# Fewer transposes for returning maxima, an earlier slot table and x, and late work moved between VectorE and GpSimd

## The chip, the cores and the metric

The kernel runs on one core of a Trainium2 chip. The engines are TensorE (matmuls and transposes, PE in the profile, with PEld its weight loads), VectorE (DVE), ScalarE (ACT), GpSimd (POOL) and SyncE (SP, which here only issues transfers). The metric is the device time of one execution in microseconds; less is better. Three executions of the kernel before took 757.74, 759.35 and 760.75 us (median 759.35).

## The reference

Masked attention with locality-sensitive buckets, followed by a mixture of experts with one expert per token. B, H, S, D = 4, 8, 768, 64; the experts see 3072 tokens of 512 values, 8 experts, hidden width 1024.

```python
q_bits = (einsum('bhsd,dk->bhsk', q, proj) > 0)        # 6 signs; bucket = their number; k likewise
mask   = q_bucket[..., :, None] == k_bucket[..., None, :]
scores = where(mask, q @ k.T / sqrt(D), -1e9)
scores = scores - max(scores, -1)
attn   = exp(scores) / (sum(exp(scores), -1) + 1e-9)
x      = (attn @ v), heads side by side                # 3072 x 512
logits = x @ w_gate + modality_bias[modality_id]
e      = argmax(logits);  gate = softmax(logits)[e]
out    = gate * (relu(x @ w1[e]) @ w2[e])              # per token, with its own expert
```

## The kernel before

**Attention.** The 32 heads are done as 16 pairs of two. For each pair, `turn` transposes q and k, `signs` multiplies them by the projection and compares, so that 12 extra rows beside the 64 of each operand carry the bucket mask, and `residues` splits the operands for two-pass products. `maxp` takes the maximum of each query's row of scores: three matmuls per tile pair and head write the banks of `psm` (two of them), VectorE reduces each (L346, L352). Queries lie in six tiles of 128. After the second tile pair (four tiles) and after the third (two tiles), L360 gathers the maxima, ScalarE spreads each over 32 columns (L363), and a closure for `maxp_back` is put into the list `late`.

`maxp_back` (L371 to L378) turns the maxima back, so that they lie along the columns of the operand: one transpose for each query tile (L374), then one instruction per head (L377) that adds them to 12 rows of the operand, and one (L378) that writes `lone`, the flag of a query that no key matches. Of each 32 rows of the spread, two halves of REP = 16 are filled for two heads. `lone` is a tile of the pool `flags`, two buffers. `vsums` writes a small matrix `vs`, which multiplied by `lone` gives the mean of v to lone queries (L457, the first instruction of each pair's `weigh`).

`score` makes the scores (L410, L411), the exponentials on ScalarE (L430, L444) and running sums over the key tiles (L447): on GpSimd, but for the second head of pair 15 (`spd=(15,)`), which is on VectorE. `weigh` multiplies by v (L463). `sums` adds the running sums over partitions (L486) one pair later, and `finish`, once for each of the four batches, makes reciprocals, router logits and the routing table (`tab`, by GpSimd's scatters, L784). `finish_x` writes x to DRAM, six tiles per batch, each four transposes (L548), a scaling on VectorE (L550) and a store (L552).

TensorE's order is written by hand: for each pair and each of six key tiles there is a string of letters (PLAN, PLAN0 for pair 0, LAST for pair 15). S is a score step, M a maximum step, T turn or signs, R residues, A two key tiles of weighing, B one call from `late`, Q the row sums of the pair before, v and V the sums of v, F, f, e, E steps of `finish`, x and y one tile of `finish_x` (x in pairs 6, 10, 14, y in pairs with i % 4 == 3). The other engines' orders come from a scheduler that takes, at each moment of its model, the earliest-written instruction that is ready. In pair 0 the orders of VectorE, ScalarE and GpSimd are also by hand (FIRST).

**Seam.** In pair 15, at its second key tile, `early_slots` (L833) works out on VectorE which two slots of 496 tokens of batches 0 to 2 can be done first; it works in a PSUM tile of `ps_x`. Then the experts' part begins: `gather` (L936) reads the slot's rows of `tab` (L941), clamps the token numbers on GpSimd (L947) and issues four indirect gathers of x (L949). `load` (L919, L923) reads the expert's weights in eight pieces of 512 KB, into four buffers, the first behind the last x store of batch 2. `split` makes each piece into an upper half (ScalarE, L929) and its residue (L933): on VectorE, but for odd pieces below 8, on GpSimd. `xprep` turns the gathered tokens (L967, four columns of four transposes each; two columns before and two behind the last weighing), copies them (L970) and takes their residues (L974). `gemm1` (L985 to L987) and `gemm2` (L1026 to L1028) follow, with batch 3's `finish` woven in.

**Experts.** After the two early slots come four more big ones, a small one and a tiny one, and the results are scattered to `out` (L1096).

Of the kernel before, what the change touches and what calls it, by code (L numbers as in the profile page):

```python
# [31 lines left out]

GROUP = 2
# [27 lines left out]
def host_consts():  # L61
    thr = np.zeros((4, 32, 3, 2), np.float32)
    for g in range(4):
        for t in range(3):
            query = (t != g // 2) if t < 2 else g % 2 == 0
            thr[g, 0:6 if query else 0, t, 0] = -TINY
            thr[g, 6:6 if query else 12, t, 0] = -TINY
            thr[g, :, t, 1] = -BIG if query else 1.0
    return {
        "c_thr": thr.reshape(128, 6),  # L70
        "c_id": np.eye(128, dtype=np.float32),
        "c_tri": np.triu(np.ones((128, 128), np.float32), 1),
    }
# [20 lines left out]
def attention(ctx, actx, tc, a, x_d, l_d, route=None, setup=None, before_last=None):  # L94
# [18 lines left out]
    flags = actx.enter_context(tc.tile_pool(name="flags", bufs=2))  # L113
# [34 lines left out]
    thr = const.tile([P, 6], F32, name="thr")  # L148
    nc.scalar.dma_start(out=thr, in_=a["c_thr"])
    load(0, (1,))  # L150
# [181 lines left out]
    def maxp(i, late, heads=(0, 1)):  # L332
# [4 lines left out]
        if "lone" not in t:  # L337
            t["lone"] = flags.tile([P, S], F32R, name="lone")
        mx = sm.tile([P, NT, nh, 2], F32, name=f"mx{nh}")
        for qt in range(0, NT, 2):  # L340
# [27 lines left out]
            late.append(partial(maxp_back, t, heads, rows, nm, n, slice(first * P, (qt + 2) * P)))  # L368
            yield

    def maxp_back(t, heads, rows, nm, n, cs):  # L371
# [17 lines left out]
    def vsums(i):  # L389

        a2, vs, share = st[i]["va"], vsb[i % 2], 1.0 if i else REP / 32
        vp = ps_x.tile([P, MAIN], F32, name="psx")
        nc.tensor.matmul(vp[:, 0:P], ones32, a2.rearrange("p h d -> p (h d)"), start=True, stop=True)
        for h in range(2):
            r = slice(64 * h, 64 * h + 64)
            nc.scalar.mul(vs[r, r], vp[r, r], share)
        for h in range(2):
            r = slice(64 * h, 64 * h + 64)
            lo = slice(64 * h + 32, 64 * h + 64)
            nc.vector.scalar_tensor_tensor(out=vs[lo, r], in0=vp[lo, r], scalar=share, in1=vs[lo, r].bitcast(F32), op0=ALU.mult, op1=ALU.subtract)  # L400
# [12 lines left out]
    def score(i):  # L413
# [22 lines left out]
        for kt in range(NT):  # L436
# [8 lines left out]
            if kt > 0:  # L445
                for h in range(2):
                    marks["add"] = (nc.vector if h and i in CFG["spd"] else nc.gpsimd).tensor_tensor(out=t["sp"][:, h], in0=(t["pb"][0] if kt == 1 else t["sp"])[:, h], in1=pb[:, h], op=ALU.add).ins  # L447
            yield

    def weigh():  # L450

        for i in range(NPR):
            t = st[i]
            t["u"] = [ps_u.tile([P, MAIN], F32, name=f"psu{j}") for j in range(2)]
            for part in range(2):
                w = COLS[part].stop - COLS[part].start
                nc.tensor.matmul(t["u"][part][:, 0:w], vsb[i % 2], t["lone"][:, COLS[part]], start=True, stop=False, skip_group_check=True)  # L457
# [128 lines left out]
    with tc.manual_schedule(engines={mybir.EngineType.PE}):  # L586
# [23 lines left out]
        for i in range(NPR):  # L610
# [8 lines left out]
            for kt in range(NT):  # L619
                if i == NPR - 1 and kt == 1:  # L620
                    before_last(ps_x.tile([P, MAIN], F32, name="psx"))
# [3 lines left out]
                for c in (PLAN0 if i == 0 else LAST if i == NPR - 1 else PLAN)[kt]:  # L625
# [30 lines left out]
                    elif c == "x" and i % 4 == 2 or c == "y" and i % 4 == 3:  # L656
# [38 lines left out]
def router(ctx, tc, a, x_d, tab):  # L695
# [137 lines left out]
    def early_slots(sp):  # L833
# [51 lines left out]
def experts(ctx, tc, a, x_d, tab, out, ps_x, idents, fold, marks):  # L885
# [40 lines left out]
    def split(r, n):  # L926
# [6 lines left out]
        (nc.gpsimd if n < 8 and n % 2 else nc.vector).tensor_tensor(out=lo, in0=r, in1=hi.bitcast(F32), op=ALU.subtract)  # L933
        return hi, lo

    def gather(s):  # L936
# [4 lines left out]
        nc.sync.dma_start(out=tb[:, 0:n], in_=tab[bass.ds(o, n * P), :].rearrange("(a p) w -> p a w", p=P))  # L941
# [10 lines left out]
    def xprep(s, xg, dst):  # L952
# [11 lines left out]
        for c in range(4):  # L964
# [9 lines left out]
            nc.vector.tensor_tensor(out=xl[:, c, 0:SL], in0=tp[:, 0:SL], in1=xh[:, c, 0:SL].bitcast(F32), op=ALU.subtract)  # L974
# [222 lines left out]
def body(tc, a, out):  # L1197
# [4 lines left out]
    with ExitStack() as ctx, ExitStack() as actx:  # L1202
        route, early_slots, late_slots, setup = router(ctx, tc, a, x_d, tab)
        finish, finish_x, ps_x, idents, fold, marks = attention(ctx, actx, tc, a, x_d, None, route, setup, lambda sp: eslot.append(early_slots(sp)))
# [41 lines left out]
```

## Time and profile before

| | us |
|---|---|
| median of 3 executions | 759.35 |
| the profiled execution | 760.22 |
| its span, first to last instruction | 758.1 |
| TensorE busy (modelled) | 738.9 |
| VectorE busy | 499.9 |
| GpSimd busy | 440.9 |
| ScalarE busy | 363.8 |

The span has three parts: the start up to about 50 us, the pairs up to about 450 us, the experts after that. Engine times are sums over the span, so they say nothing of one part alone; the timeline gives each instruction's start, length and, in brackets, the idle time before it and what ended that. [...]

### The profile page before, as it was taken

How to read it: one execution, taken by the hardware profiler on the slowest of the kernel's cores; microseconds unless marked ns; L12 is line 12 of the kernel's file. 1: busy time of each engine (PE TensorE's matmuls, PEld its weight loads, DVE VectorE, ACT ScalarE, POOL GpSimd, SP SyncE). 2: the span in 40 equal slices, each digit the busy share in tenths (PEclk: the TensorE clock that was granted, in tenths of full speed). 3: DMA queues.
4: the chain of work that ended last, by engine and by line, in shares of the span. 5: the costliest groups of instructions: out<-in, count | busy, mean ns of one | idle time of the engine just before them, and what ended most of it. 6: DMA issues, size and time to landing. Idle time of an engine off the chain costs nothing.

```text
span 758.1 us, 12219 instructions
## 1 busy us (share of the span) xinstructions
PE 738.9 (97%) x4308; PEld 523.4 (69%) x4308; DVE 499.9 (66%) x878; ACT 363.8 (48%) x649; POOL 440.9 (58%) x339
## 2 busy tenths in 40 slices
PE   6899999999999999999999999999999999999995
PEld 3556576566666657666666656888888877788884
DVE  6997779789877887977987877654343442334423
ACT  5446565555555555556465454343343432424333
POOL 8598779769888769887869984712222202202011
PEclk9999999999999999999999999999999999999998
DMA  9464455345676435664324163556544764434332
GB/s 187 116 142 109 113 122 140 83 106 116 111 131 162 105 91 133 121 157 124 92 69 85 61 199 112 115 207 185 159 137 139 250 214 147 141 123 139 96 113 82
DMA packets 105832, 99.26 MB, mean 131 GB/s; under 512 B 62594, under 2 KB 82978, under 8 KB 105760
## 3 DMA queue, kind: packets, MB, share of 16 engines
q1 hardware_dynamic: 99616, 83.79, 43.6%
q0 software_dynamic: 4832, 12.94, 4.9%
q10 hardware_dynamic: 1312, 1.65, 0.9%
q8 instruction: 36, 0.59, 0.4%
q14 instruction: 36, 0.29, 0.2%
HBM read 59.33 MB, written 12.94 MB: 95 GB/s over the span
## 4 chain that ended last, share of the span: by engine, by line
PE 81%; issue 9%; DMA 3%; POOL 2%; SPq 1%; DVE 1%; ACT 1%; POOLq 0%; ACTq 0%
PE psu L463 17%; PE pss L410 9%; PE pss L411 8%; PE psm L344 5%; PE hps L985 5%; PE hps L986 5%; PE hps L987 5%; PE yps L1026 4%; PE yps L1027 4%; PE yps L1028 4%; PE psm L350 3%; PE psx L303 2%; PE psx L486 2%; PE psx L548 2%; PE psu L220 1%
## 5 line engine op out<-in xcount | busy, mean ns | idle before, releaser
L447 POOL TENSOR_TENSOR sp<-sp,pb 128x768 f32<-128x768 f32 x124 | 225.3, 1851 | 14.1 <-ACT pb L444 13.4
L346 DVE TENSOR_REDUCE mx<-psm 128x1 f32<-128x512 f32 x192 | 130.0, 687 | 22.2 <-PE psm L344 19.1
L430 ACT ACTIVATE pb<-pss 128x512 f32<-128x512 f32 x186 | 111.5, 600 | 58.7 <-PE pss L411 50.2
L463 PE MATMUL psu<-pb,vt 128*64 128x512 f32 (+1 forms) x768 | 136.1, 497 | 0.0
L933 DVE TENSOR_TENSOR w<-raw,w 128x1024 fp32r<-128x1024 f32 x52 | 66.9, 1287 | 97.9 <-ACT w L929 97.3
L463 PEld LDWEIGHTS psu<-pb,vt 128*64 128x64 f32 x768 | 51.3, 137 | 70.6 <-issue 60.9
L929 ACT CAST w<-raw 128x1024 fp32r<-128x1024 f32 x56 | 58.5, 1047 | 81.4 <-PE yps L1028 76.7
L444 ACT ACTIVATE pb<-pss 128x512 f32<-128x512 f32 x93 | 55.6, 598 | 82.3 <-PE pss L411 80.0
L1096 POOL DMA_INDIRECT out<-y,tb x25 | 24.6, 984 | 104.1 <-ACT y L1095 100.4
L447 POOL TENSOR_TENSOR sp<-pb,pb 128x768 f32<-128x768 f32 x31 | 56.2, 1835 | 45.2 <-ACT pb L444 45.2
L1026 PE MATMUL yps<-w,hl 128*128 128x512 f32 x200 | 79.5, 397 | 0.0
L1027 PE MATMUL yps<-w,hh 128*128 128x512 f32 x200 | 78.1, 391 | 0.0
L1028 PE MATMUL yps<-w,hh 128*128 128x512 f32 x200 | 78.0, 390 | 0.0
L949 POOL DMA_INDIRECT xg<-x_d,tb x17 | 18.4, 1084 | 98.1 <-DMA tb<-tab 94.4
L985 PE MATMUL hps<-xh,w 128*128 128x496 f32 x192 | 74.4, 388 | 0.0
L986 PE MATMUL hps<-xl,w 128*128 128x496 f32 x192 | 73.8, 384 | 0.0
L987 PE MATMUL hps<-xh,w 128*128 128x496 f32 x192 | 73.8, 384 | 0.0
L410 PE MATMUL pss<-m_0g,s_0g 128*128 128x512 f32 (+1 forms) x186 | 69.2, 372 | 0.0
L991 DVE SCALAR_TENSOR_TENSOR hl<-hps,hh 128x496 fp32r<-128x496 f32 x48 | 32.4, 674 | 53.0 <-ACT hh L990 52.9
L352 DVE TENSOR_REDUCE mx<-psm 128x2 f32<-128x512 f32 x96 | 66.1, 688 | 1.0
L410 PE MATMUL pss<-m_1g,s_1g 128*128 128x512 f32 (+1 forms) x186 | 65.7, 353 | 0.2 <-ACT pb L430 0.2
L990 ACT ACTIVATE hh<-hps 128x496 fp32r<-128x496 f32 x48 | 28.1, 585 | 78.5 <-PE hps L987 76.1
(267 smaller groups left out, 1419.7 us busy)
## 6 DMA issues: line engine op xcount, KB each, us to landing
raw<-moe_w SPq DMA_DIRECT2D x56, 512.0 KB
vt<-v SPq DMA_DIRECT2D x16, 384.0 KB
qk<-q SPq DMA_DIRECT2D x31, 192.0 KB
qk<-k SPq DMA_DIRECT2D x31, 192.0 KB
x_d<-xs SPq DMA_DIRECT2D x18, 256.0 KB
tw<-moe_w SPq DMA_DIRECT2D x2, 2048.0 KB
m_0g<-m_0g SPq DMA_DIRECT2D x16, 192.0 KB
s_0g<-s_0g SPq DMA_DIRECT2D x16, 192.0 KB
```

Source lines behind the costliest of these rows:

```text
L346: marks["m"] = nc.vector.tensor_reduce(out=mx[:, qt + j, hi, 0:1], in_=mp, axis=AX.X, op=ALU.max).ins
L410: nc.tensor.matmul(out, t["s1"][h][:, ks], t["m1"][h][:, cs], start=True, stop=False)
L430: marks["p"] = nc.scalar.activation(t["pb"][kt][:, h, 0:MAIN], sp, AF.Exp, scale=0.125).ins
L447: marks["add"] = (nc.vector if h and i in CFG["spd"] else nc.gpsimd).tensor_tensor(out=t["sp"][:, h], in0=(t["pb"][0] if kt == 1 else t["s ...
L463: marks["u", kt] = nc.tensor.matmul(t["u"][part][64 * h:64 * h + 64, 0:w], t["v"][:, h, kt], t["pb"][kt][:, h, COLS[part]], start=False, s ...
L933: (nc.gpsimd if n < 8 and n % 2 else nc.vector).tensor_tensor(out=lo, in0=r, in1=hi.bitcast(F32), op=ALU.subtract)
L985: nc.tensor.matmul(hps, lo[:, c, fs], xh[:, c, 0:SL], start=(c == 0), stop=False)
L986: nc.tensor.matmul(hps, hi[:, c, fs], xl[:, c, 0:SL], start=False, stop=False)
L987: nc.tensor.matmul(hps, hi[:, c, fs], xh[:, c, 0:SL], start=False, stop=(c == 3))
L1026: nc.tensor.matmul(yps[g], hl[fc][:, gs], hi[:, fb], start=(fc == 0), stop=False)
L1027: nc.tensor.matmul(yps[g], hh[fc][:, gs], lo[:, fb], start=False, stop=False)
L1028: nc.tensor.matmul(yps[g], hh[fc][:, gs], hi[:, fb], start=False, stop=(fc == 7))
```

## The change

The diff has three parts.

First, the returning maxima. ScalarE's spread L363 now fills 16 of each 32 columns once per tile and head, so that one tile of 128 columns holds two query tiles, and `maxp_back` makes one transpose for two of them. Rows 0 to 63 then carry one tile and rows 64 to 127 the other. For two heads there is one addition per head and tile parity u (four, each over every second tile) and one flag instruction per u; pair 0, which does its heads one by one, keeps its transposes and its addition and has two flag instructions of 32 rows. `lone` becomes two fixed tiles that GpSimd clears at the start, and `vsums` uses four columns `pick` that come with the thresholds' constant (10 columns instead of 6). `vsb` isn't cleared any more.

Second, `early_slots` is called in pair 14 at key tile EARLY_AT = 1, on a tile of its own in SBUF, and the letter y also writes x tiles in pair 14, so that all six of batch 2 are written there. The table rows of the first early slot are asked for behind the last x store of batch 2 on the same queue.

Third, in pair 15 all running sums but the first of head 0 are on VectorE, all residues of the weights are on VectorE, and ordering hints put the last two running sums behind the first two columns' token residues, and the residues of pieces 1 to 3 behind the fourth column's.

```diff
@@ host_consts
+    pick = np.zeros((2, 2, REP, 2, 2), np.float32)
+    for h in range(2):
+        pick[h, 0, :REP // 2, 1, h] = 1.0
+        pick[h, 0, REP // 2:, 1, h] = -1.0
+        pick[h, 0, REP // 2:, 0, h] = 1.0
...
@@ attention
+    lone = [const.tile([P, S], F32R, name=f"lone{j}") for j in range(2)]
-    spread_to = {(j, n): const.tile([P, n, P], F32R, name=f"nm{n}_{j}") for j in range(2) for n in (4, 2)}
+    spread_to = {(j, n): const.tile([P, n // 2, P], F32R, name=f"nm{n}_{j}") for j in range(2) for n in (4, 2)}
...
-        nc.gpsimd.memset(ones32, 1.0 / REP)
-        for vs in vsb:
-            nc.gpsimd.memset(vs.bitcast(F32), 0.0)
+        nc.gpsimd.memset(ones32, 2.0 / REP)
+        for z in lone:
+            nc.gpsimd.memset(z.bitcast(F32), 0.0)
@@ maxp
-                nc.scalar.mul(nm.rearrange("p j (g w) -> p (j g) w", w=32)[:, :, 0:REP].rearrange("p (x r) w -> p x r w", r=2),
-                              m.rearrange("p j h -> p (j h)").unsqueeze(2).unsqueeze(3).broadcast_to([P, 2 * n, 2, REP]), -1.0 / 6)
+                nc.scalar.mul(nm.rearrange("p a (x w) -> p (a x) w", w=32)[:, :, 0:REP], m.rearrange("p j h -> p (j h)").unsqueeze(2).broadcast_to([P, 2 * n, REP]), -1.0 / 6)
@@ maxp_back
-        for j in range(n):
-            nc.tensor.transpose(bc.bitcast(F32R)[:, j * P:(j + 1) * P], nm[:, j] if len(heads) == 2 else nm[:, j].broadcast_to([P, P]), identr)
-        for h in heads:
-            to = slice(64 * h, 64 * h + NB)
-            nc.vector.scalar_tensor_tensor(out=t["m1"][h][to, cs], in0=bc[to, 0:n * P], scalar=BIG / 16, in1=t["m1"][h][to, cs].bitcast(F32), op0=ALU.min, op1=ALU.add)
-        nc.vector.tensor_scalar(out=t["lone"][rows, cs], in0=bc[rows, 0:n * P], scalar1=BIG / 16, scalar2=None, op0=ALU.is_gt)
+        one = len(heads) == 1
+        for j in range(n if one else n // 2):
+            nc.tensor.transpose(bc.bitcast(F32R)[:, j * P:(j + 1) * P], nm[:, j].broadcast_to([P, P]) if one else nm[:, j], identr)
...
+        for h in () if one else heads:
+            for u in range(2):
+                to = t["m1"][h][64 * h:64 * h + NB, cs].rearrange("p (a u c) -> p a u c", u=2, c=P)[:, :, u]
+                at = 64 * u + 32 * h
+                nc.vector.scalar_tensor_tensor(out=to, in0=value(slice(at, at + NB), u), scalar=BIG / 16, in1=to.bitcast(F32), op0=ALU.min, op1=ALU.add)
+        for u in range(2):
+            for at in [64 * u + 32 * h for h in heads][:2 if one else 1]:
+                rows = slice(at, at + (32 if one else 64))
+                to = lone[i % 2][rows, cs].rearrange("p (a u c) -> p a u c", u=2, c=P)[:, :, u]
+                nc.vector.tensor_scalar(out=to, in0=value(rows, u), scalar1=BIG / 16, scalar2=None, op0=ALU.is_gt)
@@ score
-                    marks["add"] = (nc.vector if h and i in CFG["spd"] else nc.gpsimd).tensor_tensor(...).ins
+                    marks["add"] = (nc.vector if i == NPR - 1 and (h or kt > 1) else nc.gpsimd).tensor_tensor(...).ins
+                    marks["add", kt, h] = marks["add"]
@@ the loop over pairs
-                if i == NPR - 1 and kt == 1:
-                    before_last(ps_x.tile([P, MAIN], F32, name="psx"))
+                if i == NPR - 2 and kt == EARLY_AT:
+                    before_last()
...
-                    elif c == "x" and i % 4 == 2 or c == "y" and i % 4 == 3:
+                    elif c == "x" and i % 4 == 2 or c == "y" and (i % 4 == 3 or i == NPR - 2):
@@ early_slots
+        sp = const.tile([P, 96], F32, name="esp")
@@ split
-        (nc.gpsimd if n < 8 and n % 2 else nc.vector).tensor_tensor(out=lo, in0=r, in1=hi.bitcast(F32), op=ALU.subtract)
+        sub = nc.vector.tensor_tensor(out=lo, in0=r, in1=hi.bitcast(F32), op=ALU.subtract)
+        if 0 < n < 4:
+            after(sub.ins, marks["xl"])
@@ gather
+        if s == ("e", 0):
+            after(got.ins, marks["x", B - 2])
@@ xprep
+            if s == ("e", 0) and c == 3:
+                marks["xl"] = sub.ins
+            if s == ("e", 0) and c == 1:
+                for h in range(2):
+                    after(marks["add", NT - 1, h], sub.ins)
```

## Rows read from the trace of the kernel before

**Rows 1.** page, busy time (us, share of the span, instructions) of each engine

```profile
PE 738.9 (97%) x4308; PEld 523.4 (69%) x4308; DVE 499.9 (66%) x878; ACT 363.8 (48%) x649; POOL 440.9 (58%) x339
```

**Rows 2.** stretches: length, then each engine's busy us (instructions); last, clock, DMA share, GB/s

```profile
60.00:430.00 370.00, 370.00 (x2435) 241.07 (x2431) 299.68 (x546) 205.65 (x397) 303.29 (x197) 1.00 0.48 111
...
455.00:457.00 2.00, 2.00 (x8) 0.49 (x4) 1.38 (x2) 1.01 (x2) 1.92 (x2) 0.50 0.00 0
```

**Rows 3.** timeline of TensorE at the seam: start, us, instruction [idle before <-releaser]

```profile
446.69 2.80 PE L463 MATMUL psu<-pb,vt 128*64 128x512 f32 x16
...
450.00 0.22 PE L967 MATMUL psx<-identr,xg 128*128 128x128 f32 x1
...
451.11 0.28 PE L967 MATMUL psx<-identr,xg 128*128 128x128 f32 x1 [0.90 <-DMA xg<-x_d,at]
...
452.93 4.49 PE L463 MATMUL psu<-pb,vt 128*64 128x512 f32 x16
...
457.35 0.87 PE L967 MATMUL psx<-identr,xg 128*128 128x128 f32 x8
```

**Rows 4.** timeline of the start: TensorE, GpSimd

```profile
24.41 0.50 PE L350 MATMUL psm<-s_1g,m_1g 128*128 128x256 f32 x2 [0.88 <-DVE mx L346]
...
15.76 0.20 POOL L597 COPY gst<-wg 64x32 f32<-64x32 f32 x1 [2.12 <-DMA wg<-moe_w_gate]
```

**Rows 5.** timeline of TensorE, one turn back of four tiles, whole and cut off

```profile
291.44 0.46 PE L374 MATMUL psx<-identr,nm 128*128 128x128 f32 x4
...
291.56 0.34 PE L374 MATMUL psx<-identr,nm 128*128 128x128 f32 x2
```

**Rows 6.** groups by form: busy us, mean ns | idle before, releaser

```profile
L378 DVE TENSOR_SCALAR lone<-psx 128x512 fp32r<-128x512 f32 x15 | 10.4, 692 | 0.2
...
L378 DVE TENSOR_SCALAR lone<-psx 128x256 fp32r<-128x256 f32 x15 | 6.4, 425 | 0.2
...
L530 DVE TENSOR_TENSOR gl<-psx,rin 128x128 f32<-128x128 f32 x4 | 1.2, 289 | 1.3 <-PE psx L529 1.3
```

**Rows 7.** timeline of VectorE behind the weighing at a pair's end

```profile
294.96 0.41 DVE L377 SCALAR_TENSOR_TENSOR m_0g<-psx,m_0g 12x256 fp32r<-12x256 f32 x1 [0.56 <-PE psx L374]
...
297.78 0.69 DVE L346 TENSOR_REDUCE mx<-psm 128x1 f32<-128x512 f32 x1 [0.93 <-PE psm L344]
```

**Rows 8.** timeline of VectorE in pair 15, first and last of the table

```profile
431.95 0.20 DVE L799 TENSOR_TENSOR sg<-psx,kstep 128x48 f32<-128x48 f32 x1
...
438.15 0.16 DVE L831 TENSOR_SCALAR eslot<-psx 128x2 int32<-128x2 f32 x1
```

**Rows 9.** timeline of pairs 14 and 15: VectorE, GpSimd, TensorE

```profile
422.49 0.68 DVE L550 TENSOR_TENSOR xs<-psx,rin 128x512 f32<-128x512 f32 x1
...
423.47 14.35 POOL L447 TENSOR_TENSOR sp<-sp,pb 128x768 f32<-128x768 f32 x8
...
441.37 0.23 POOL L947 TENSOR_SCALAR at<-tb 128x4 int32<-128x4 int32 x1 [1.51 <-DMA tb<-tab]
...
442.41 1.08 POOL L949 DMA_INDIRECT xg<-x_d,at  x1 [0.80 <-POOL at L947]
...
443.79 1.72 POOL L949 DMA_INDIRECT xg<-x_d,at  x1 [0.30 <-issue]
...
447.29 1.17 POOL L949 DMA_INDIRECT xg<-x_d,at  x1 [0.30 <-issue]
...
441.51 0.85 PE L486 MATMUL psx<-sp,ones 128*32 128x384 f32 x8
```

**Rows 10.** timeline of the seam: VectorE, ScalarE, GpSimd

```profile
443.70 0.96 DVE L447 TENSOR_TENSOR sp<-sp,pb 128x768 f32<-128x768 f32 x1 [0.72 <-ACT pb L444]
...
448.58 2.83 DVE L933 TENSOR_TENSOR w<-raw,w 128x1024 fp32r<-128x1024 f32 x1 [0.95 <-ACT w L929]
...
453.63 2.00 ACT L929 CAST w<-raw 128x1024 fp32r<-128x1024 f32 x2
...
457.41 5.75 POOL L933 TENSOR_TENSOR w<-raw,w 128x1024 fp32r<-128x1024 f32 x2
```

More of the change, by code (lines that the diff above doesn't have):

```diff
@@ L31 @@
 P = 128
+EARLY_AT = 1
 GROUP = 2
@@ L147, in attention @@
     nc.scalar.activation(warm, warm, AF.Exp)
-    thr = const.tile([P, 6], F32, name="thr")
+    thr = const.tile([P, 10], F32, name="thr")
     nc.scalar.dma_start(out=thr, in_=a["c_thr"])
+    pick = thr[:, 6:10]
     load(0, (1,))
@@ L367, in maxp, with maxp_back, value @@
                 nc.vector.tensor_scalar(out=nm, in0=m, scalar1=-1.0 / 6, scalar2=None, op0=ALU.mult)
-            late.append(partial(maxp_back, t, heads, rows, nm, n, slice(first * P, (qt + 2) * P)))
+            late.append(partial(maxp_back, i, heads, rows, nm, n, slice(first * P, (qt + 2) * P)))
             yield
-    def maxp_back(t, heads, rows, nm, n, cs):
+    def maxp_back(i, heads, rows, nm, n, cs):
+        t = st[i]
         bc = ps_x.tile([P, MAIN], F32, name="psx")
-        for j in range(n):
-            nc.tensor.transpose(bc.bitcast(F32R)[:, j * P:(j + 1) * P], nm[:, j] if len(heads) == 2 else nm[:, j].broadcast_to([P, P]), identr)
-        for h in heads:
-            to = slice(64 * h, 64 * h + NB)
-            nc.vector.scalar_tensor_tensor(out=t["m1"][h][to, cs], in0=bc[to, 0:n * P], scalar=BIG / 16, in1=t["m1"][h][to, cs].bitcast(F32), op0=ALU.min, op1=ALU.add)
-        nc.vector.tensor_scalar(out=t["lone"][rows, cs], in0=bc[rows, 0:n * P], scalar1=BIG / 16, scalar2=None, op0=ALU.is_gt)
+        one = len(heads) == 1
+        for j in range(n if one else n // 2):
+            nc.tensor.transpose(bc.bitcast(F32R)[:, j * P:(j + 1) * P], nm[:, j].broadcast_to([P, P]) if one else nm[:, j], identr)
+        def value(rows, u):
+            return bc[rows, 0:n * P].rearrange("p (a u c) -> p a u c", u=2, c=P)[:, :, u] if one else bc[rows, 0:n // 2 * P].rearrange("p (a c) -> p a c", c=P)
+        if one:
+            to = t["m1"][heads[0]][64 * heads[0]:64 * heads[0] + NB, cs]
+            nc.vector.scalar_tensor_tensor(out=to, in0=bc[64 * heads[0]:64 * heads[0] + NB, 0:n * P], scalar=BIG / 16, in1=to.bitcast(F32), op0=ALU.min, op1=ALU.add)
+        for h in () if one else heads:
[8 more added lines that the diff above has]
+                nc.vector.tensor_scalar(out=to, in0=value(rows, u), scalar1=BIG / 16, scalar2=None, op0=ALU.is_gt)
@@ L446, in score @@
                 for h in range(2):
-                    marks["add"] = (nc.vector if h and i in CFG["spd"] else nc.gpsimd).tensor_tensor(out=t["sp"][:, h], in0=(t["pb"][0] if kt == 1 else t["sp"])[:, h], in1=pb[:, h], op=ALU.add).ins
+                    marks["add"] = (nc.vector if i == NPR - 1 and (h or kt > 1) else nc.gpsimd).tensor_tensor(out=t["sp"][:, h], in0=(t["pb"][0] if kt == 1 else t["sp"])[:, h], in1=pb[:, h], op=ALU.add).ins
+                    marks["add", kt, h] = marks["add"]
             yield
@@ L456, in weigh @@
                 w = COLS[part].stop - COLS[part].start
-                nc.tensor.matmul(t["u"][part][:, 0:w], vsb[i % 2], t["lone"][:, COLS[part]], start=True, stop=False, skip_group_check=True)
+                nc.tensor.matmul(t["u"][part][:, 0:w], vsb[i % 2], lone[i % 2][:, COLS[part]], start=True, stop=False, skip_group_check=True)
             for kt in range(NT):
@@ L831, in assign, with early_slots @@
         nc.vector.tensor_scalar(out=out[:, 1], in0=r, scalar1=float(DUMMY), scalar2=None, op0=ALU.add)
-    def early_slots(sp):
+    def early_slots():
+        sp = const.tile([P, 96], F32, name="esp")
         out = const.tile([P, 2, EARLY], I32, name="eslot")
@@ L940, in gather @@
         tb = gp.tile([P, TS // P, 2], I32, name="tb", bufs=4)
[L941 removed]
+        got = nc.sync.dma_start(out=tb[:, 0:n], in_=tab[bass.ds(o, n * P), :].rearrange("(a p) w -> p a w", p=P))
+        if s == ("e", 0):
+            after(got.ins, marks["x", B - 2])
         xg = gp.tile([P, TS // P, DM], F32R, name="xg", bufs=XG)
@@ L1203, in body @@
         route, early_slots, late_slots, setup = router(ctx, tc, a, x_d, tab)
-        finish, finish_x, ps_x, idents, fold, marks = attention(ctx, actx, tc, a, x_d, None, route, setup, lambda sp: eslot.append(early_slots(sp)))
+        finish, finish_x, ps_x, idents, fold, marks = attention(ctx, actx, tc, a, x_d, None, route, setup, lambda: eslot.append(early_slots()))
         actx.close()
```

16 lines of the change are left out of this document (7 added, 9 removed).

## The prediction

> **What bounds the kernel now.** I read the page's busy table first. TensorE is named busy for 738.9 of 758.1 us and VectorE for 499.9 [rows 1]; since a busy TensorE is modelled, I checked with the stretches that it is really the bound. Between 60 and 430 us, where attention runs pair after pair, it is busy for 370.00 of 370.00 us while VectorE, ScalarE and GpSimd have 299.68, 205.65 and 303.29 [rows 2]. The timeline of TensorE there shows starts one behind the other with no named wait, so in that stretch an instruction taken out of its stream is time taken out of the kernel, and an instruction added to VectorE costs nothing as long as it falls into a gap.
>
> The chain of waits then leads to one place where TensorE does stand: the seam between attention and the experts. At 450.00 us the first turn of the first slot's gathered tokens starts and the next ones must wait, 0.90 us at 451.11; the eight turns take until 452.93, 2.93 us. [...] The third place is the start, where TensorE waits for VectorE's maxima (0.88 us at 24.41) [rows 4].
>
> **The change, part by part.** The sum is made against the profiled execution's own 760.22 us (758.1 us span and 2.1 around it), 0.87 above the median 759.35.
>
> *One turn for two query tiles.* For pairs 1 to 15, maxp_back issues half its transposes: 6 become 3 per pair, 45 in all. Four of them start at 291.44, and the last two are seen from 291.56: 0.06 us each [rows 5]. 45 x 0.06 = 2.7 us off TensorE. Lower end 0 (TensorE then waits for another), upper end 0.115 us each, the four's whole 0.46 us over four [rows 5], so 5.2 us. I take 2.7.
>
> The price is on VectorE. A call had 3 instructions over all columns and now has 6 over half of them: 0.69 us at 512 columns, 0.42 at 256, 0.29 at 128 [rows 6]. The call for four tiles goes from 3 x 0.69 = 2.07 to 6 x 0.42 = 2.52 us, the one for two tiles from 3 x 0.42 = 1.26 to 6 x 0.29 = 1.74: +0.93 us per pair. The cover is VectorE's own gaps at this very place: 0.56 us before the second call's work and 0.93 before the next maxima [rows 7]. 0.45 fits into the one, 0.48 into the other, so I take 0. Without the cover it costs 15 x 0.93 = 14.0 us; below nothing it can't go, since no VectorE work leaves. The narrower copy on ScalarE (half of 256 and 128 columns) gains some 0.1 us off the path. In vsums the two scalings and two combinations stay at the same column count, on more partitions: 0.
>
> *Start.* Pair 0's four calls get one instruction more each (two strided halves of 32 rows for one of 64): 2 x (2 x 0.42 - 0.69) + 2 x (2 x 0.29 - 0.42) = 0.62 us on VectorE [rows 6], and here TensorE does wait for it [rows 4]. I take 0.6 us lost (0 to 1.3, the upper end if the new length of pair 1's first call is paid too). The flags' buffers become fixed tiles that GpSimd clears, and it no longer clears `vsb`; it stands 2.12 us at 15.76 for a transfer [rows 4], which hides it.
>
> *Early slots, x and the rows.* early_slots moves from pair 15's second step to pair 14's, and the last three tiles of x with it (12 transposes, no change for TensorE's sum). VectorE thereby gets in pair 14 three scalings of 0.68 us, the table's 18 small instructions (the first 0.20 us at 431.95, the last 0.16 at 438.15 [rows 8], so some 3.2 us) and 0.93 from above, 6.2 us; in that pair it has no residues or signs to make, since no pair 16 follows. Over the pairs it is free 19% of the time [rows 2], 5 us of a pair's 26, in bursts while TensorE weighs. I let 0.3 us of the chain reach TensorE (0, if all falls into bursts, to 3.2).
>
> What it brings: at present the table's last instruction ends at 438.31, GpSimd waits for its rows until 441.37, and the four gathers run until 448.46 [rows 8, 9] and land after 450 [rows 3]. With slots known a pair earlier, the rows are asked for behind pair 14's last x tile, whose scaling starts at 422.49 [rows 9]; with the present 3.1 us from table to rows they are there by 427, and the gathers can end 5 to 15 us sooner. Then at 450.00 all eight turns go at the pace of rows 5, 8 x 0.06 = 0.5 us instead of 2.93, and the weighing behind them takes 2.80 instead of 4.42, since TensorE hasn't stood: 2.4 + 1.6 = 4.0 us gained [rows 3, 5]. Lower end 0, upper end 4.0.
>
> *VectorE alone for residues and late adds.* Four adds of pair 15 and the residues of weight pieces 1, 3, 5, 7 go from GpSimd to VectorE. Now GpSimd's two residues take 5.75 us from 457.41 and VectorE's own first one 2.83 us while GpSimd adds; an add on VectorE takes 0.96 alone [rows 10]. After: six adds at 0.96 and a residue well under 2.83 before the turns, two adds and three residues behind. The first products need piece 0 and the token halves; with TensorE 4 us earlier, the halves of columns 2 and 3 are next late, because ScalarE has two casts (2.00 us [rows 10]) and two copies between them. I take 0.4 us lost (0 to 2). Pieces 5 and 7 lie beside TensorE's own work: 0.
>
> *What is late next.* The gathers' 5.8 us are put into GpSimd's queue: the index's 0.23 and four times the first gather's 1.08 with the 0.30 ahead of one [rows 9]. There pair 14's last eight adds run from 423.47 to 437.8, and TensorE needs them at 441.51 for the row sums: 3.7 us in hand [rows 9]. If gathers go in ahead of the last adds, which is likely because GpSimd is free whenever the schedule thinks the next exponentials aren't done, the sums wait 5.8 - 3.7 - 0.3 (TensorE is already that much later) = 1.8 us. Bounds: 0, if they stand behind the adds, and 5.8 if nothing of the slack is left.
>
> [...] In the trace one took 1.72 us and began 0.09 us after a VectorE add; the first, with no add beside it, took 1.08 [rows 9, 10]. [...]
>
> Sum: -2.7 + 0.6 + 0.3 - 4.0 + 0.4 + 1.8 = -3.6 us: 756.6 for an execution like the profiled one, 755.75 from the median.
>
> **Rivals.**
>
> *Gathers behind the adds.* Without the wait at the row sums the sum is -5.4: 753.95. For it: now the scheduler lets them follow all adds of pair 14 and one of pair 15 [rows 9]. Against: now their rows aren't there before.
>
> *The seam stays as long.* The gathers end in time, but the products then wait for VectorE's halves or residues, or the gathers come no sooner since they are put behind all of GpSimd's adds and land at 450 as now. For it: VectorE gets some 8 us of adds and residues between 440 and 458, more than the three adds and two residues it has there now. Then only -2.7 + 0.6 + 0.3 = -1.8 remains: 757.55.
>
> *VectorE takes over as the bound of the pairs (slower).* Place: the end of each pair, from the second call's work to the next maxima. If the schedule puts the six instructions ahead of the maxima that free TensorE's banks, what exceeds the gaps is paid by every pair. Price: the whole 14.0 us, so 759.35 + 14.0 + 0.6 - 2.7 - 3.6 = 767.65. It decides from (2.7 + 3.6 - 0.6) / 15 = 0.38 us per pair upward. For it: VectorE is busy 81% of the stretch [rows 2], and half the pairs carry finishing work that fills gaps. Against: the two gaps above.
>
> **How the numbers follow.** The forecast has 0.45, gathers behind the adds 0.25, the seam as long 0.20, VectorE the bound 0.10. 0.5% is 3.8 us, about what a measurement of this kernel can tell from no change: faster means under 755.55, which is just below the forecast. Of the forecast I count half (0.22) as faster, of gathers behind the adds 0.85 (0.21), of the others none: 0.43. Slower gets 0.09 of the last. The rest, 0.48, is the same. Range: the first rival with a free start and half of what the transposes' upper end adds (0.6 and 1.3) gives 752.05, the seam rival with the 1.8 us wait at the sums 759.35: 752.0 to 759.6. The last rival is left out.
>
> **What would show it.** Right: 45 transposes fewer in the group of maxp_back, and pairs 0.18 us shorter; no wait at the first slot's turns and a granted clock of 1.00 through the seam, the first product 4 us closer to the weighing before it; table rows read near 426 instead of 441; a wait of 1 to 2 us before pair 14's row sums, released by GpSimd. Wrong: waits of the maxima's matmuls for VectorE in the pairs (slower rival), a wait of the first products for VectorE's halves or residues (seam as long), or row sums without a wait (gathers behind the adds).

## The result: slower, and the profile after

Before 759.13 us median of 6 runs (757.57 to 761.47), after 766.49 (764.75 to 768.31): ratio 1.0097, 95% interval 1.0081 to 1.0114. The forecast was 755.75 in a range of 752.0 to 759.6, so it had the wrong sign. The profiled execution after took 766.73 us, its span 764.9.

| | before | after |
|---|---|---|
| span, us | 758.1 | 764.9 |
| row sums of pair 0 | 67.89 | 69.62 |
| row sums of pair 12 | 392.60 | 393.06 |
| row sums of pair 13 | 417.58 | 429.73 |
| row sums of pair 14 | 441.51 | 452.07 |
| row sums of pair 15 (the seam lies before them) | 459.80 | 466.62 |

The table holds the start of TensorE's row sums (`psx<-sp,ones`) as its timeline gives them. The sums of a pair run in the next one, so the stretch from pair 12's sums to pair 13's reaches into pair 14, where the early table now is. Differences line by line: start +1.73, the twelve pairs up to pair 12's sums -1.27, the stretch up to pair 13's +11.69, the next -1.59, seam -3.74, the rest 0; together +6.8, the difference of the spans. So one stretch, at the head of pair 14, lost more than everything else moved. Some 1.6 us of its 11.69 are work that moved in from the stretch behind it, which is as much shorter; the turns of two x tiles are among it.

The page's busy row and the stretches of the kernel after, in the columns of [rows 1, 2]:

```profile
PE 737.2 (96%) x4263; PEld 520.6 (68%) x4263; DVE 523.7 (68%) x980; ACT 363.5 (48%) x649; POOL 421.7 (55%) x331
```

```profile
60.00:430.00 370.00, 360.16 (x2337) 230.94 (x2337) 311.65 (x627) 200.44 (x388) 297.84 (x193) 0.99 0.48 112
60.00:392.00 332.00, 331.31 (x2164) 212.14 (x2162) 277.49 (x562) 187.88 (x362) 269.48 (x172) 1.00 0.50 115
392.00:430.00 38.00, 28.85 (x175) 18.80 (x175) 34.16 (x66) 12.56 (x26) 28.36 (x22) 0.91 0.38 84
...
455.00:457.00 2.00, 2.00 (x13) 1.73 (x12) 2.00 (x4) 2.00 (x5) 0.00 (x0) 1.00 0.00 0
```

TensorE executes 45 instructions fewer, as foretold, and yet the stretch that had no idle time now has 10 us of it, nearly all between 392 and 430, where the mean granted clock (TensorE's, as a share of its full speed) is 0.91. At the seam it is the other way round: 1.00 where it was 0.50. The waits of TensorE after, between 400 and 470 us (engine, what it writes, line, what it waited for: us in total, times, longest), name the place:

```profile
PE psx L569 <- DVE vs L420: 8.8, 1, 8.8
PE psm L356 <- DVE mx L352: 0.3, 1, 0.3
```

`vs` at L420 is two innocent instructions of 0.46 us together. The timeline of VectorE shows what stood ahead of it in its queue:

```profile
408.86 1.61 DVE L820 TENSOR_TENSOR sg<-esp,kstep 128x48 f32<-128x48 f32 x1
...
413.44 8.70 DVE L850 TENSOR_TENSOR esp<-esp,selx 128x16 f32<-128x16 f32 x1
422.06 0.15 DVE L842 CAST eslot<-esp 128x2 int32<-128x2 f32 x1
...
422.45 0.20 DVE L852 TENSOR_SCALAR eslot<-esp 128x2 int32<-128x2 f32 x1
422.56 0.46 DVE L420 SCALAR_TENSOR_TENSOR vs<-psx,thr,vx 128x64 fp32r<-128x64 f32 x2
```

A multiplication of 16 columns took 8.70 us. GpSimd's timeline beside it:

```profile
413.11 0.95 POOL L805 DMA_INDIRECT tab<-rec,posi  x1 [0.30 <-issue]
414.08 3.57 POOL L467 TENSOR_TENSOR sp<-sp,pb 128x768 f32<-128x768 f32 x2
417.59 3.56 POOL L467 TENSOR_TENSOR sp<-pb,pb 128x768 f32<-128x768 f32 x2
421.11 0.98 POOL L404 TENSOR_TENSOR va<-vt 128x384 f32<-128x384 f32 x1
422.17 0.45 POOL L405 TENSOR_TENSOR va<-va 128x128 f32<-128x128 f32 x1
```

Five additions follow one another without a break from 414.08 to 422.09, and the multiplication ends at 422.14. In the kernel before, the same chain of small instructions (the early table) ran beside eight such additions (423.47 to 437.82, [rows 9]) at 0.16 to 0.23 us an instruction. One instruction of it was slow even there, and it is the only one with two inputs in SBUF; the neighbour that reads the chain's scratch (`psx`, a tile of PSUM) is not:

```profile
434.58 1.47 DVE L860 SCALAR_TENSOR_TENSOR eb<-early,wbase 128x8 f32<-128x8 f32 x1
435.98 0.17 DVE L817 TENSOR_TENSOR psx<-psx,selx 128x16 f32<-128x16 f32 x1
```

The change had moved that scratch from PSUM to SBUF: `before_last(ps_x.tile(...))` became `sp = const.tile([P, 96], F32, name="esp")`. The diff shows it; the prediction passed over it.

The seam, to be held beside [rows 3]: eight turns without a wait, and the weighing behind them takes 2.80 us like the one ahead of them.

```profile
457.42 2.80 PE L484 MATMUL psu<-pb,vt 128*64 128x512 f32 x16
460.73 0.79 PE L993 MATMUL psx<-identr,xg 128*128 128x128 f32 x8
461.45 2.80 PE L484 MATMUL psu<-pb,vt 128*64 128x512 f32 x16
464.18 0.86 PE L993 MATMUL psx<-identr,xg 128*128 128x128 f32 x8
```

### The profile page after: what moved, and what is told of

The parts are those of the page before. It is cut to its first block, busy times and chain, and to the rows that moved or that the text cites. A ratio compares the mean times of both kernels' runs of the same rounds, so it can differ in the third digit from the quotient of the medians.

```text
span 764.9 us, 12211 instructions
## 1 busy us (share of the span) xinstructions
PE 737.2 (96%) x4263; PEld 520.6 (68%) x4263; DVE 523.7 (68%) x980; ACT 363.5 (48%) x649; POOL 421.7 (55%) x331
## 4 chain that ended last, share of the span: by engine, by line
PE 80%; issue 10%; DVE 7%; DMA 1%; POOL 1%; ACT 1%; SPq 0%; POOLq 0%; ACTq 0%; DVEq 0%
PE psu L484 16%; PE pss L430 9%; PE pss L431 8%; PE psm L350 5%; PE hps L1016 5%; PE hps L1018 5%; PE hps L1017 5%; PE yps L1057 4%; PE yps L1058 4%; PE yps L1059 4%; PE psm L356 3%; PE psx L311 3%; PE psx L507 2%; DVE mx L352 2%; PE psu L228 1%
## 5 line engine op out<-in xcount | busy, mean ns | idle before, releaser
L467 POOL TENSOR_TENSOR sp<-sp,pb 128x768 f32<-128x768 f32 x120 | 217.2, 1846 | 21.0 <-ACT pb L464 20.5
L484 PE MATMUL psu<-pb,vt 128*64 128x512 f32 (+1 forms) x768 | 134.4, 492 | 0.0
```

The costliest lines, as they stand in the source:

```text
L467: marks["add"] = (nc.vector if i == NPR - 1 and (h or kt > 1) else nc.gpsimd).tensor_tensor(out=t["sp"][:, h], in0=(t["pb"][0] if kt == 1 ...
L484: marks["u", kt] = nc.tensor.matmul(t["u"][part][64 * h:64 * h + 64, 0:w], t["v"][:, h, kt], t["pb"][kt][:, h, COLS[part]], start=False, s ...
```

## Experiments

Theory A: the scratch in SBUF makes instructions of VectorE wait for GpSimd's additions, and that is the 8.70 us. Rivals: the table's new place in pair 14 costs, wherever its scratch lies; the first part (one turn for two tiles) takes VectorE's gaps away.

| kernel | median, us | ratio to before, 95% |
|---|---|---|
| after, scratch back in PSUM | 759.72 | 0.9992 to 1.0033 |
| before, scratch in SBUF | 770.71 | 1.0123 to 1.0184 |
| first part alone | 759.31 | 1.0001 to 1.0031 |
| after without the first part | 757.01 | 0.9963 to 0.9993 |
| after, additions behind the table's multiplication | 765.90 | 1.0079 to 1.0119 |
| after, additions behind the whole table | 757.37 | 0.9967 to 0.9993 |
| first part alone, flags cleared on VectorE | 758.78 | 0.9995 to 1.0021 |
| without the first part, gathers behind pair 14's sums | 755.05 | 0.9941 to 0.9969 |
| after, additions behind the table, gathers behind the sums | 755.90 | 0.9951 to 0.9981 |

The kernel before had 758.44 us beside the first four of these, 758.83 beside the two with the additions behind the whole table, and 758.23 beside the other three. Each kernel ran 4 to 10 times.

### The scratch back in PSUM

```
-                    before_last()
+                    before_last(ps_x.tile([P, MAIN], F32, name="psx"))
-    def early_slots():
-        sp = const.tile([P, 96], F32, name="esp")
+    def early_slots(sp):
```

> The changed kernel with one thing undone: the early table's scratch is a PSUM tile again, at the same place in pair 14; VectorE's order is the same. Theory A (the scratch in SBUF gives the table's instructions two SBUF inputs, and one of them waits until GpSimd's run of adds breaks): the instruction of 8.7 us takes about 0.2, TensorE's wait of 8.82 us in pair 14 goes with the half clock behind it, and the time falls by some 10 us, to 756 to 757 us (before: 759.1, changed: 766.5). Theory B (the place is at fault: VectorE has too much to do in pair 14, whatever the operands): at most 3 us go, 763 us or more. A smaller rival of A: the tile holds one of two banks of psx for some 5 us, and TensorE waits 1 to 4 us for it, 757 to 760.

759.72 us: most of the loss is gone, and no instruction of the table lasts over 0.23 us. What is left is another wait, which the chain in PSUM brings at this place: it holds one of the two `psx` banks that the x tiles need (row of TensorE).

```profile
416.46 1.12 PE L569 MATMUL psx<-ident,ut 128*128 128x128 f32 x4 [2.91 <-DVE xs L571]
```

So a PSUM scratch has a price at this place too, about a third of the SBUF scratch's; it is the smaller rival of theory A.

### The kernel before with only the scratch moved

```
-                    before_last(ps_x.tile([P, MAIN], F32, name="psx"))
+                    before_last()
-    def early_slots(sp):
+    def early_slots():
+        sp = const.tile([P, 96], F32, name="esp")
```

> The kernel before with one thing done: the early table's scratch in SBUF, at its old place in pair 15. Theory A: some instructions of the table with two SBUF inputs last until GpSimd's adds of pair 14 break, which is at about 437.8 to 440 us there; single ones of 1.5 to 6 us are to be seen instead of 0.17, and the sums of v behind them on VectorE are late: 760 to 764 us. Theory B: nothing changes, 758.5 to 760.

770.71 us, 1.5% slower by one tile's memory, and above the 760 to 764 that I expected. With the scratch in SBUF the scheduler also put the chain forward in VectorE's order, into pair 14 (that the PSUM bank had held it back is not shown), where it met the same run of GpSimd: the same 8.70 us, and TensorE's wait behind it is 9.78.

```profile
412.23 8.70 DVE L829 TENSOR_TENSOR esp<-esp,selx 128x16 f32<-128x16 f32 x1
```

None of the change's other parts is in this kernel, so none of them is needed for the loss.

### The first part alone

Only `maxp`, `maxp_back`, `vsums`, the fixed flag tiles and the constants of the change.

> The kernel before with the first part of the change alone (one turn for two query tiles, the fixed flags, the columns pick). By the prediction 757 us (-2.7 in the pairs, +0.6 at the start). By the trace of the changed kernel, which is 1.7 us late at the row sums of pair 0 and wins 0.10 us per pair after that: 759.1 + 1.7 - 1.5 = 759.3, no difference. If VectorE's instructions cost more than that, 760 or more.

759.31 us, no difference to speak of. Pair 0's row sums start at 68.83 instead of 67.89 (+0.94), those of pair 12 at 392.27 instead of 392.60: the twelve pairs between take 323.44 instead of 324.71 us, 0.11 less each. What the shorter turns give there, the start takes.

### Everything but the first part

> The changed kernel without its first part. Theory A: the long instruction of the table stays (1.5 to 9 us, by where GpSimd's adds break), and the time is about that of the changed kernel less its loss up to pair 13: 765 to 766 us. Theory B (VectorE is overfull in pair 14 by the six instructions of each turn back): the wait in pair 14 shrinks by half or more, 757 to 761 us.

757.01 us: my expectation of a slow kernel failed. The scratch is in SBUF here, and yet the longest instruction of the table took 1.89 us. VectorE's and GpSimd's timelines say why:

```profile
407.02 1.89 DVE L806 TENSOR_TENSOR sc<-esp,klow 128x64 f32<-128x64 f32 x1
...
411.15 0.17 DVE L831 TENSOR_TENSOR esp<-esp,selx 128x16 f32<-128x16 f32 x1
...
411.68 0.17 DVE L833 TENSOR_SCALAR eslot<-esp 128x2 int32<-128x2 f32 x1
```

```profile
405.18 3.63 POOL L448 TENSOR_TENSOR sp<-sp,pb 128x768 f32<-128x768 f32 x2
408.97 0.98 POOL L786 DMA_INDIRECT tab<-rec,posi  x1 [0.17 <-issue]
410.26 0.96 POOL L786 DMA_INDIRECT tab<-rec,posi  x1 [0.31 <-issue]
411.53 0.96 POOL L786 DMA_INDIRECT tab<-rec,posi  x1 [0.30 <-issue]
412.51 3.63 POOL L448 TENSOR_TENSOR sp<-sp,pb 128x768 f32<-128x768 f32 x2
```

The one instruction that fell beside additions ended with them (408.91 and 408.81). The rest of the chain fell beside GpSimd's scatters and was through 0.7 us before the next additions began. Held against GpSimd's last scatter ahead of the additions, the multiplication starts 0.38 us before it here (411.15 and 411.53) and 0.33 us behind it in the kernel after (413.44 and 413.11). Between these two kernels, the 0.7 us go with the difference between 0.17 and 8.70 us. Nothing in this kernel keeps the chain and the additions apart; that they missed each other is luck.

### Measuring the wait by itself

```
+                if 2 <= i < 14 and kt in (1, 4):
+                    n = 2 * (i - 2) + kt // 4
+                    behind(nc.vector.tensor_tensor(out=two[:, n], in0=probe[:, 0:16], in1=probe[:, 16:32], op=ALU.add).ins, marks["m"])
+                    behind(nc.vector.tensor_reduce(out=one[:, n:n + 1], in_=probe[:, 0:16], axis=AX.X, op=ALU.add).ins, marks["m"])
```

> The kernel before with 48 small instructions added on VectorE, behind the last maxima of key tiles 1 and 4 in pairs 2 to 13: 24 additions of 16 columns whose two inputs both lie in SBUF (two<-probe), and 24 row sums of the same 16 columns, with one input in SBUF (one<-probe). Nothing that the kernel computes depends on them. Theory A (a VectorE instruction with two SBUF inputs waits while GpSimd's additions read SBUF, whatever its own size): the additions last 0.17 us where GpSimd is idle or computes nothing, and up to 2 us behind one addition of GpSimd or 4 us behind two where it adds, always ending when GpSimd's run ends; the row sums last 0.17 us everywhere. Theory B (the 8.70 us belong to the table's own chain, for instance its operand's layout or its place behind ScalarE): the additions last 0.17 us like the row sums.

The view by tile (ns: shortest, median, longest), for the two kinds:

```profile
L626 DVE TENSOR_TENSOR two<-probe x24: 165/1385/3827, 82.5 to 409.1; 128x16 f32<-128x16 f32 x24
```

```profile
L627 DVE TENSOR_REDUCE one<-probe x24: 152/155/161, 83.4 to 410.3; 128x1 f32<-128x16 f32 x24
```

All additions but one waited (0.35 us and more), and each wait ended with an addition of GpSimd. But my expectation that it would always be the last one of GpSimd's run failed: 20 of the 23 waits ended with the addition beside which they had begun, and in 11 of these the next addition followed without a break. The one at 98.55 begins beside the second of six back-to-back additions (96.12 to 106.91) and ends with it, at 99.80:

```profile
98.55 1.25 DVE L626 TENSOR_TENSOR two<-probe 128x16 f32<-128x16 f32 x1
```

```profile
96.12 10.79 POOL L447 TENSOR_TENSOR sp<-sp,pb 128x768 f32<-128x768 f32 x6 [0.68 <-ACT pb L444]
```

Three lasted through a second addition, such as the one at 334.97: it ends at 337.05, with the last of six (337.01). The one run of this kernel took 771.57 us: against 758.23 for the kernel before beside it, the 48 small instructions cost some 13.

### GpSimd's additions behind the table's multiplication

```
+        if n == EARLY:
+            seen = wk.tile([P, 1], F32, name="seen")
+            tail.append(nc.gpsimd.tensor_copy(out=seen, in_=sel[:, 0, 0:1]).ins)
...
                     before_last()
+                    for h in range(2):
+                        behind(marks["add", NT - 1, h], tail[0], "the sums follow the early table")
```

> The changed kernel with one order added: the last two additions of pair 13's running sums on GpSimd wait for the early table's last instruction with two SBUF inputs (a copy of one column on GpSimd, about 0.2 us, reads its output). The scratch stays in SBUF, the table stays where the change put it, and VectorE's order is the same. Theory A (the 8.70 us are a wait for GpSimd's run of four additions and a fifth): that instruction lasts 0.2 us instead of 8.70, pair 14 is 9 to 11 us shorter, time 755.5 to 758.5 us. Theory B (the place in pair 14 itself costs, because the value transposes' scaling queues behind the table's chain on VectorE): pair 14 stays over 30 us long and the time 764 to 767 us.

765.90 us, which is theory B's number. The multiplication did become short, but the wait turned up three instructions later, at one with a single input in SBUF (VectorE; GpSimd adds from 414.48 on):

```profile
413.70 0.18 DVE L853 TENSOR_TENSOR esp<-esp,selx 128x16 f32<-128x16 f32 x1
413.82 0.17 DVE L845 CAST eslot<-esp 128x2 int32<-128x2 f32 x1
414.02 0.17 DVE L857 TENSOR_REDUCE esp<-esp 128x2 f32<-128x16 f32 x1
414.23 8.30 DVE L858 TENSOR_SCALAR eslot<-esp 128x2 int32<-128x2 f32 x1
```

Either the place itself costs, or theory A had named one kind of instruction too few. The next two tell these apart.

### Additions behind the whole table, and a second probe

```
         nc.vector.tensor_scalar(out=out[:, 1], in0=r, scalar1=float(DUMMY), scalar2=None, op0=ALU.add)
+        if n == EARLY:
+            seen = wk.tile([P, 1], I32, name="seen")
+            tail.append(nc.gpsimd.tensor_copy(out=seen, in_=out[:, 1, 0:1]).ins)
```

> The changed kernel with the same order as in the run that ordered two additions behind the table's multiplication, one step further: the last two additions of pair 13's running sums on GpSimd wait for the very last instruction of the early table, the 128x2 conversion to integers, which has one SBUF input and took 8.30 us in that run while GpSimd's four additions and a fifth ran. Theory A (GpSimd's run of additions holds off a VectorE instruction of either kind: two SBUF inputs, or one input and one output in SBUF for an operation of tensor_scalar's kind): no table instruction lasts over 2 us, TensorE's wait of 8.4 us for the value sums goes, pair 14 is 9 to 11 us shorter, time 755.5 to 758.5 us. Theory B (the place in pair 14 costs whatever holds VectorE): the wait turns up at a third instruction and the time stays at 764 to 767 us.

757.37 us. Same scratch, same place, same order on VectorE; GpSimd starts its additions 0.28 us behind its last scatter (414.62 to 414.90) instead of at once, and all is well: the last instruction takes 0.17 us, TensorE waits 0.28 us for `vs` instead of 8.82.

```profile
414.51 0.17 DVE L855 TENSOR_SCALAR eslot<-esp 128x2 int32<-128x2 f32 x1
414.60 0.48 DVE L421 SCALAR_TENSOR_TENSOR vs<-psx,thr,vx 128x64 fp32r<-128x64 f32 x2
```

```profile
415.23 0.63 PE L570 MATMUL psx<-ident,ut 128*128 128x128 f32 x4 [0.28 <-DVE vs L421]
```

The multiplication, too, answers a question here. It starts 0.33 us behind the start of GpSimd's last scatter, just as in the kernel after, and takes 0.17 us. So the scatter doesn't hold it; what differs is the addition that GpSimd has next:

```profile
413.99 0.17 DVE L853 TENSOR_TENSOR esp<-esp,selx 128x16 f32<-128x16 f32 x1
```

```profile
413.66 0.96 POOL L808 DMA_INDIRECT tab<-rec,posi  x1 [0.30 <-issue]
```

From pair 12's row sums to pair 13's it takes 26.59 us, against 36.67 after. Of these 10.1 us, 8.5 are the wait (8.82 less 0.28); the rest goes with the granted clock, 0.91 from 392 to 430 after and 1.00 here.

The second probe has 24 additions of a constant to 2 columns (`tensor_scalar`, float to integer, both in SBUF) in place of the two-input ones.

> The kernel before with 48 small instructions added on VectorE at the places of the earlier probe: 24 additions of a constant to 2 columns, one input in SBUF, output integers in SBUF (the form of the table's last instruction), and 24 row sums of the same 2 columns, also one SBUF input. Nothing computed depends on them. Theory A (that form waits for GpSimd's additions although it has one SBUF input): 0.17 us where GpSimd pauses, up to 4 us behind its additions, median 1 us or more as for the probe with two SBUF inputs (1.385 us); the row sums 0.15 us everywhere. Theory B (only two SBUF inputs wait, and the 8.30 us came from elsewhere): both 0.15 to 0.2 us.

```profile
L626 DVE TENSOR_SCALAR two<-probe x24: 160/1380/3860, 82.0 to 408.2; 128x2 int32<-128x2 f32 x24
```

```profile
L627 DVE TENSOR_REDUCE one<-probe x24: 136/140/150, 82.9 to 409.4; 128x1 f32<-128x2 f32 x24
```

It waits just as long as the two-input kind (medians 1380 and 1385 ns), and the row sums beside it never (150 ns at most); its 23 waits end in the same way, 20 of them with the addition beside which they began. Theory A holds in the wider form.

### What the gathers ahead of the additions cost

```
+                    if i == NPR - 2:
+                        marks["add14"] = marks["add"]
...
-            nc.gpsimd.tensor_scalar(out=at, in0=tb[:, :, 0:1], scalar1=(B - 1) * S - 1, scalar2=None, op0=ALU.min)
+            cap = nc.gpsimd.tensor_scalar(out=at, in0=tb[:, :, 0:1], scalar1=(B - 1) * S - 1, scalar2=None, op0=ALU.min)
+            after(cap.ins, marks["add14"])
```

> The changed kernel without its first part (two maxima tiles in one turn), and with the first early slot's four gathers ordered behind pair 14's running sums on GpSimd. Against the kernel without the first part alone (757.01 us) it tells what the gathers ahead of the additions cost: there TensorE waited 0.50 and 0.92 us at pair 14's row sums for GpSimd's additions. Theory A (that wait is on the path, and the gathers have time to land): the two waits go, the first slot's turns start when they did, time 755 to 756.3 us. Theory B (the gathers now land too late, as in the kernel before): a wait of 1 us or more at the turns of the first slot's tokens, time 757 to 759 us.

755.05 us against 757.01 without the edit; by the two ratios (0.9978 and 0.9955) 1.7 us, though their intervals overlap a little. Without it TensorE waited twice at pair 14's row sums:

```profile
440.56 0.84 PE L488 MATMUL psx<-sp,ones 128*32 128x384 f32 x4 [0.50 <-POOL sp L448]
442.31 0.84 PE L488 MATMUL psx<-sp,ones 128*32 128x384 f32 x4 [0.92 <-POOL sp L448]
```

With it the gathers start at 436.38 instead of 433.09, the row sums go in one piece at 440.02, and the first slot's turns still find their tokens: TensorE's timeline from 436 to 465 names no wait.

### The start, and both mends together

```
-        for z in lone:
-            nc.gpsimd.memset(z.bitcast(F32), 0.0)
...
+    for z in lone:
+        nc.vector.memset(z.bitcast(F32), 0.0)
```

> The first part of the change alone (two maxima tiles in one turn), with the two flag tiles cleared on VectorE before its first copies instead of on GpSimd ahead of the first signs. Against the first part alone (759.31 us; first maxima at 10.29 us in its profile, pair 0's row sums at 68.89). Theory A (the 1.42 us of clearing on GpSimd cost the start about 1 us): first maxima at 9.2 to 9.9, time 757.8 to 758.7 us. Theory B (the start is set by pair 0's extra flag instructions on VectorE, not by the clearing): first maxima earlier but pair 0's row sums still at 68.5 or later, time 758.9 to 759.8 us.

758.78 us, between the two expectations and inside the interval of the first part alone. In the profiled execution the first maxima start at 10.58 and pair 0's row sums at 68.98, no earlier than before the edit; but its granted clock was 0.50 from 20.2 to 23.6, which it wasn't without the edit. Inconclusive.

> The changed kernel with that order, and with the first early slot's gathers ordered behind pair 14's running sums. It is the kernel without the first part but with the gathers behind (755.05 us, the fastest so far) plus the first part of the change. Theory A (the first part is worth 1.3 us over 13 pairs and costs about 1 us in pair 0): 754 to 756 us, no difference from 755.05 that the runs can tell. Theory B (the first part costs more than it gives, as its single run of 759.31 us against 758.44 suggests): 756 to 757.5 us.

755.90 us, 0.9951 to 0.9981 of before (the 13 pairs of the expectation are twelve). With both mends the change is a small gain; the first part adds nothing to it that the runs can tell (0.9941 to 0.9969 without it).

## Why the prediction was wrong

**The step that failed** is the term of the early table: "I let 0.3 us of the chain reach TensorE (0, if all falls into bursts, to 3.2)". It measured 10.1 us: the stretch from pair 12's row sums to pair 13's in the kernel after, against the same kernel with GpSimd's additions behind the table. The chain's instructions were priced by rows whose scratch lies in PSUM [rows 8], though the change puts it into SBUF; the upper bound, the chain's whole busy time, was no bound, since the wait of one instruction came on top of it. And what queued behind it on VectorE, `vs` for the value sums, had TensorE waiting. The trace of the kernel before held two signs: the chain's one instruction with two SBUF inputs at 1.47 us (the prediction counts 18 instructions, the trace has 19), and VectorE's residue at 2.83 us beside GpSimd's additions [rows 10] (a residue of the same size in the kernel after, at 460.40, where GpSimd stands: 1.21).

What the runs measured of that wait: for two inputs in SBUF a median of 1385 ns, for one input and an integer output in SBUF 1380, against 155 and 140 ns for the row sums at the same places (the two probes). Mostly a wait was the rest of one addition, but in the kernel after it went on through five additions, 8.70 us. The prediction looked at what VectorE's additions do to the gathers, and not at what GpSimd's additions do to the instructions whose operand moved.

**Rival "VectorE takes over as the bound of the pairs"** had the right sign and the wrong mechanism. The twelve pairs between the first two lines of the table did get shorter, and the loss sits at the head of pair 14. VectorE's gaps took the longer flags only in part, as the next term shows.

**One turn for two tiles**, -2.7: the right sign, mis-sized, and its price on VectorE, taken as 0, was not 0. 45 turns went, but a pair is 0.11 us shorter instead of 0.18. In the first part alone, over the same twelve pairs and from start to next start on TensorE, the turns back take 4.01 us instead of 7.09, for 36 turns fewer: more than the 0.06 each that I took. But the step from a score to the q and k turns behind it, 36 times, takes 11.22 us instead of 8.42. At one of these places the flags end at 296.61 instead of 296.24, and the turn starts behind them, 0.40 us after the score instead of 0.23. Before, and with the first part alone (TensorE, then VectorE):

```profile
296.68 0.40 PE L411 MATMUL pss<-m_1g,s_1g 128*128 128x512 f32 x1
296.91 0.60 PE L303 MATMUL psx<-ident,qk 128*128 128x128 f32 x4
```

```profile
296.27 0.40 PE L430 MATMUL pss<-m_1g,s_1g 128*128 128x512 f32 x1
296.67 0.66 PE L310 MATMUL psx<-ident,qk 128*128 128x128 f32 x4
```

```profile
296.02 0.59 DVE L397 TENSOR_SCALAR lone<-psx 64x128 fp32r<-64x128 f32 x2
```

In the groups by line after, the weight loads of these turns stand 4.3 us for the flags, which they did not before.

```profile
L311 PEld LDWEIGHTS psx<-ident,qk 128*128 128x128 f32 x168 | 19.7, 140 | 10.4 <-DVE lone L398 4.3 <-PE pss L431 2.1 <-PE pss L430 0.4
```

**Start**, +0.6 (0 to 1.3): +0.94 with the first part alone, +1.73 in the profiled execution after. Up to 27 us these two are level (a maxima's matmul starts at 27.09 and 27.05); then the granted clock is 0.50 for 3.4 us in the kernel after, and 1.00 in the first part alone, and there the other 0.8 us come up:

```profile
27.10:30.50 3.40, 3.40 (x9) 2.44 (x9) 2.50 (x6) 0.70 (x2) 1.97 (x4) 0.50 0.10 22
```

In all profiles of this record, pair 0's row sums start between 66.60 and 67.89 without the first part and between 68.79 and 70.24 with it. The clearing of the flags, which I priced at nothing, lies ahead of the first signs on GpSimd; moving it gave no clear gain, so how the loss divides stays open.

**Seam**, -4.0 + 0.4: measured -3.74, with no wait at the turns, the weighing at 2.80 us instead of 4.42, and a granted clock of 1.00 instead of 0.50. Right; with both mends, where pair 14 isn't late, it is -3.88. VectorE's residues and additions, the seam rival's reason, did not hold TensorE up: it names no wait between 424 and 470.

**Gathers ahead of the additions**, +1.8: 1.7 us between the two kernels that differ in nothing else, 1.4 by the two waits. Right; in the kernel after itself TensorE names no wait at these sums, since it comes to them so late.

With 10.1 in place of 0.3, -1.3 for the turns, +0.9 for the start, -3.7 for the seam and nothing for the row sums, the sum is +6.0 us. With the 0.8 us of the half clock at the start of that one execution it is the +6.8 of the profiled spans; the medians differ by 7.4.

## What to carry to other kernels

Read in a diff where each operand lives before and after. Here a tile that moved from PSUM to SBUF changed what its instructions waited for, though their number, size and engine stayed the same: beside GpSimd's additions, the multiplication by `selx` took 0.18 us in the kernel before (at 437.21) and 8.70 after. Where a small VectorE instruction with two SBUF inputs, or a `tensor_scalar` from SBUF to integers in SBUF, waited in these runs, it cost from the rest of one GpSimd addition (the probes' medians are 1.4 us) up to GpSimd's whole unbroken run at that place (8.70 us), and then what queued behind it. If such an instruction can't leave that place, make GpSimd's run begin behind it, and behind the chain's last instruction of either kind: here 0.3 us of delay there bought 10 us on TensorE.

## What the runs showed that I had not expected

- How long a wait lasts is not settled. In each probe 20 of 23 ended with the addition beside which they began, 11 of them although the next one followed at once. So did the 1.47 us in the kernel before: they ended at 436.05, while GpSimd's eight additions ran on to 437.82. The longest, 8.70 us through five additions and 8.30 in the variant, both began just ahead of a run's first addition, 0.64 and 0.25 us by the record. What lets VectorE in between two additions, and what doesn't, no run here shows.
- In the kernel after, VectorE came in at a break of 0.08 us between two of GpSimd's instructions (422.09 to 422.17).
- GpSimd's scatters (`DMA_INDIRECT`, 0.96 us) did not hold the same instructions up: 0.17 us each beside them. The exceptions had a run of additions right behind the scatter, as the multiplication in the kernel after.
- One input in SBUF was no protection for `tensor_scalar` to integers (up to 3.86 us in the probe, 8.30 in the table); a reduction over the same columns never took more than 0.161 us.
